# Laying the inputs of a Fourier-plus-experts kernel out in the order in which it loads them

## The chip, the cores and the metric

The kernel runs on one core of a Trainium2 chip. The metric is the device time of one execution in microseconds (us), as the median of several runs without a profile. A profiled execution gives the page and the trace from which the views below are read; its times are us from the start of its span unless they are marked ns.

## What is computed

A two-dimensional Fourier transform over sequence and channels, of which the real part is kept, and then a mixture of experts in which each token goes to one expert. Cut to what matters:

```python
# x: (8, 2496, 256), w_gate: (256, 8), w1: (8, 256, 1024), w2: (8, 1024, 256), all float32
X = np.fft.fft(x, axis=1)
X = np.fft.fft(X, axis=2)
t = X.real.astype(np.float32).reshape(8 * 2496, 256)      # 19968 tokens

logits = t @ w_gate
expert = np.argmax(logits, axis=1)
gate = softmax(logits)[token, expert]
for e in range(8):                                        # every token to its own expert
    h = np.maximum(t[expert == e] @ w1[e], 0.0)
    y[expert == e] = h @ w2[e]
out = gate[:, None] * y
```

## The kernel before

The sequence of 2496 is split as 104 x 24. A batch goes through these steps.

1. **First stage** (`first`). The 24 samples of a row are worked on as 12 pairs of mirrored samples in three thirds of four. For each third, `xl` (four samples) is loaded directly by SP, and `xh` (the four mirrored ones) comes by a gather from GpSimd, because the mirrored rows run backwards and need computed row numbers. VectorE adds the two, with one of them read backwards along the channels, folds the channels into a cosine and a sine half, and TensorE multiplies with `w1` waves. ScalarE copies the results out of PSUM, and SP stores them to the DRAM tensor `Td`.
2. **Regrouping** (`regroup`). Two loads per batch bring `Td` back with other rows on the partitions (120 of them), as `t4`.
3. **Second stage** (`second`). Small matmuls on `t4`, then the channel transform, which gives rows of tokens and their logits.
4. **Routing** (`route`). VectorE finds each token's expert and place; GpSimd scatters the rows to `Xs`, which is sorted by expert: ten scatters of 128 rows for each half of a batch.
5. **Experts** (`experts`). Blocks of 512, 256 or 128 rows of one expert are loaded with that expert's `w1` and `w2` (1 MB each), multiplied, and scattered to the output.

The order of instructions on each engine is written by hand: generators are woven so that the stages of batch b + 1 lie among the experts' work on batch b. Each engine does its own instructions in that order.

The parts that the change touches, with cuts marked:

```python
    ix = cp.tile([NA, B, NQ], I32, name="ix")              # row numbers for the gathers
    pool.iota(ix[:], [[S // 4, B], [-1, NQ]], base=NB // 4 * NA - 1, channel_multiplier=-(NB // 4))
    # ... cut ...
    xall = x.rearrange("b (p j) d -> (b p) j d", j=NB)
    xrows = x.rearrange("b (n j) d -> (b n) (j d)", j=4)

    def load_x(b, q):
        xl = xp.tile([NP, 4, D], F32, tag="xl", name="xl", bufs=3)      # NP = 112
        xh = xp.tile([NA, 4, D], F32, tag="xh", name="xh", bufs=3)      # NA = 104, D = 256
        n = NP if b + 1 < B else NA
        nc.sync.dma_start(out=xl[0:n], in_=xall[NA * b:NA * b + n, 4 * q + 1:4 * q + 5])
        pool.indirect_dma_start(
            out=xh[:].rearrange("p j d -> p (j d)"), out_offset=None, in_=xrows,
            in_offset=bass.IndirectOffsetOnAxis(ap=ix[:, b, q:q + 1], axis=0))
        return xl[0:NA], xh[:]

    def fold(xl, xh, q):
        n = 3 if q == NQ - 1 else 4
        a, m = xl, xh
        vec.tensor_tensor(free(a, 1, [D, n], [1, D - 1]), free(a, 1, [D, n], [1, D - 1]),
                          free(m, 3 * D + D - 1, [-D, n], [-1, D - 1]), op=ALU.add)
        yield
        vec.tensor_tensor(free(a, 0, [D, n]), free(a, 0, [D, n]), free(m, 3 * D, [-D, n]), op=ALU.add)
        fold_d(m, a, 4)
        yield

    def load(b, q):                    # the loads of third q; with q = 0 sample 0 too, as x0
        # ... cut ...

    def first(b):
        pm0 = xp.tile([NA, D], F32, tag="pm0", name="pm0")
        for q in range(NQ + 1):        # NQ = 3
            # ... first half of the fold of third q; yield ...
            # ... half of the matmuls of third q - 1; second half of the fold; yield ...
            if q:
                half1(b, q - 1, 1, pm, pm0, t1)
                nc.sync.dma_start(out=Td[b][:, 4 * (q - 1) * D:4 * q * D], in_=t1[:].rearrange("p j d -> p (j d)"))
                load(b + 1, q - 1)
            next(f, None)
            if q == 1:
                fold_d(pm0[:], ahead.pop((b, "x0")), 1)
            pm = xh
            yield

    def regroup(b, h):
        t4 = sp.tile([GP, HALF, D], F32, tag="t4", name="t4")           # GP = 120, HALF = 6
        n = min(HALF, NG - h * HALF)
        nc.sync.dma_start(
            out=t4[:, 0:n], in_=bass.AP(Td[b].tensor, Td[b].offset + h * HALF * GP * D,
                                        [[D, GP], [GP * D, n], [1, D]]))
        ahead[b, "t4", h] = t4

    # in fetch: a block's rows, then its weights, all on SP
        w1_sb = bp.tile([128, 2, F], F32, tag="w1", name="w1_sb", bufs=3)
        nc.sync.dma_start(out=w1_sb[:], in_=w1[ds(ev, 1)].rearrange("o (c p) f -> p (o c) f", p=128))
        w2_sb = bp.tile([128, FC, D], F32, tag="w2", name="w2_sb", bufs=3)
        nc.sync.dma_start(out=w2_sb[:], in_=w2[ds(ev, 1)].rearrange("o (c p) d -> p (o c) d", p=128))

    # the start of the program
    act.dma_start(out=con["w1"][:, 0:4], in_=waves[:, 0:4])
    load(0, 0)
    act.dma_start(out=con["w1"][:, 4:], in_=waves[:, 4:])
    for _ in range(WARM):              # WARM = 12 matmuls on a tile of ones
        pw = psy.tile([128, D], F32, tag="y", name="py")
        mm(pw[:], ones[:], bc(ones[:], 1, 2))
    load(0, 1)
    load(0, 2)
    act.dma_start(out=con["rt"][:], in_=const_dram("rt", consts["rt"]))
    act.dma_start(out=wg[:], in_=w_gate.rearrange("(c p) e -> p c e", p=128))
    nc.sync.dma_start(out=table[:], in_=const_dram("table", packed))
    nc.sync.dma_start(out=bt[:], in_=const_dram("blocks", cv))
    # ... cut: the rows of padding of Xs; a first Exp ...
    for _ in first(0):
        pass
    regroup(0, 0)
    regroup(0, 1)
    # ... cut: the gate's weights through the channel transform (pg) ...
    early = ahead_of(1)                # first(1), then regroup(1, 0) and regroup(1, 1)
    for _ in range(7):
        next(early)
    for k, _ in enumerate(second(0)):  # second stage and routing of batch 0
        if k % 2 == 0:
            next(early, None)
    # ... cut: experts, woven with the stages of the batches to come ...
```

Of the kernel before, what the change touches and what calls it, by code (L numbers as in the profile page):

```python
# [11 lines left out]
F32 = mybir.dt.float32  # L12
# [33 lines left out]
def free(ap, offset, *dims):  # L46
    return bass.AP(ap.tensor, ap.offset + offset, [list(ap.ap[0])] + [list(d) for d in dims])
# [122 lines left out]


TICKS = 44
WARM = 12
MOST = max(k for now in rounds() for _, k, _ in now)


# [15 lines left out]
def kernel(ctx: ExitStack, tc, x, w_gate, w1, w2, out):  # L192
# [3 lines left out]
    def mm(o, lhsT, rhs, start=True, stop=True, **kw):  # L196
        nc.tensor.matmul(o, lhsT=lhsT, rhs=rhs, start=start, stop=stop, **kw)  # L197
# [39 lines left out]
    ix = cp.tile([NA, B, NQ], I32, name="ix")  # L237
    pool.iota(ix[:], [[S // 4, B], [-1, NQ]], base=NB // 4 * NA - 1, channel_multiplier=-(NB // 4))
    pad = cp.tile([128, W], F32, name="pad")
    vec.memset(pad[:], 0.0)  # L240
    vec.memset(pad[:, D:D + 1], OUT)
# [20 lines left out]
    ident = con["ident"]  # L262
    waves = const_dram("w1", consts["w1"])


    xall = x.rearrange("b (p j) d -> (b p) j d", j=NB)
    xrows = x.rearrange("b (n j) d -> (b n) (j d)", j=4)

    def load_x(b, q):
        xl = xp.tile([NP, 4, D], F32, tag="xl", name="xl", bufs=3)  # L270
        xh = xp.tile([NA, 4, D], F32, tag="xh", name="xh", bufs=3)
        n = NP if b + 1 < B else NA
        nc.sync.dma_start(out=xl[0:n], in_=xall[NA * b:NA * b + n, 4 * q + 1:4 * q + 5])
        pool.indirect_dma_start(  # L274
            out=xh[:].rearrange("p j d -> p (j d)"), out_offset=None, in_=xrows,
            in_offset=bass.IndirectOffsetOnAxis(ap=ix[:, b, q:q + 1], axis=0))
        return xl[0:NA], xh[:]

    def fold_d(o, a, n):

# [2 lines left out]
        vec.tensor_tensor(free(o, H + 1, [D, n], [1, H - 1]), lo, hi, op=ALU.subtract)  # L283
        vec.tensor_copy(free(o, 0, [D, n], [H, 2]), free(a, 0, [D, n], [H, 2]))  # L284

    def fold(xl, xh, q):

        n = 3 if q == NQ - 1 else 4
        a, m = xl, xh
        vec.tensor_tensor(free(a, 1, [D, n], [1, D - 1]), free(a, 1, [D, n], [1, D - 1]),  # L290
                          free(m, 3 * D + D - 1, [-D, n], [-1, D - 1]), op=ALU.add)
        yield
        vec.tensor_tensor(free(a, 0, [D, n]), free(a, 0, [D, n]), free(m, 3 * D, [-D, n]), op=ALU.add)
        fold_d(m, a, 4)
        yield

# [11 lines left out]

    ahead = {}

    def load(b, q):
        if b < B:
            ahead[b, q] = load_x(b, q)
        if b < B and q == 0:
            n = NP if b + 1 < B else NA
            x0 = xp.tile([NP, D], F32, tag="x0", name="x0")
            nc.sync.dma_start(out=x0[0:n], in_=xall[NA * b:NA * b + n, 0])
            ahead[b, "x0"] = x0[0:NA]

    def first(b):  # L320

        pm0 = xp.tile([NA, D], F32, tag="pm0", name="pm0")
        for q in range(NQ + 1):
            f = iter(())
            if q < NQ:
                xl, xh = ahead.pop((b, q))
                f = fold(xl, xh, q)
# [12 lines left out]
            if q == 1:  # L340
                fold_d(pm0[:], ahead.pop((b, "x0")), 1)
            pm = xh
            yield

    base = con["cap"]

    def regroup(b, h):
        t4 = sp.tile([GP, HALF, D], F32, tag="t4", name="t4")
        n = min(HALF, NG - h * HALF)
        nc.sync.dma_start(  # L350
            out=t4[:, 0:n], in_=bass.AP(Td[b].tensor, Td[b].offset + h * HALF * GP * D,
                                        [[D, GP], [GP * D, n], [1, D]]))
        ahead[b, "t4", h] = t4

    zz = cp.tile([128, 2, NW * 128], F32, name="zz")
# [1 line left out]
    def second(b):  # L357

        t4 = None

        def turn_last(h):

            nonlocal t4
            t4 = ahead.pop((b, "t4", h))
            n = min(HALF, NG - h * HALF)
            pr = pm_.tile([GP, HALF], F32, tag="m", name="pr")
            mm(pr[:, 0:n], con["rot"][:], t4[:, 0:n, H])
            act.copy(t4[:, 0:n, H], pr[:, 0:n])

        def group(g):  # L370
            i, n = g % HALF, LAST if g == NG - 1 else GP
            p2 = pm_.tile([128, 2, n], F32, tag="m", name="p2")
            for c in range(2):
                mm(p2[:, c], t4[:, i, c * H:(c + 1) * H], con["m2"][:, c, 0:n])
# [144 lines left out]

    def turn(size, xb):  # L520
# [119 lines left out]
    act.dma_start(out=con["rt"][:], in_=const_dram("rt", consts["rt"]))  # L640
    act.dma_start(out=wg[:], in_=w_gate.rearrange("(c p) e -> p c e", p=128))
    nc.sync.dma_start(out=table[:], in_=const_dram("table", packed))
    nc.sync.dma_start(out=bt[:], in_=const_dram("blocks", cv))
    sent(unordered(nc.sync.dma_start(
        out=Xs[E * CAP:].rearrange("(k p) w -> p k w", k=BLK // 128), in_=bc(pad[:], 1, BLK // 128)), "xs"), 0)
# [5 lines left out]
    todo = in_order()  # L651
    for _ in first(0):
        pass
    regroup(0, 0)
    regroup(0, 1)
    vec.tensor_copy(tri[:], con["tri"][:])
    for c in range(2):
        pg = pm_.tile([128, E], F32, tag="m", name="pg")
# [36 lines left out]
_OUTS = [((NT, D), "float32")]  # L695


# [18 lines left out]
```

## Time and profile before

| | before |
|---|---|
| time, median of 3 runs | 1383.64 us (1382.79 to 1387.59) |
| profiled execution | 1424.57 us, span 1422.8 us |
| TensorE matmul (PE) busy | 1338.3 us (94%) |
| TensorE weight load (PEld) busy | 1016.2 us (71%) |
| VectorE (DVE) busy | 382.6 us (27%) |
| ScalarE (ACT) busy | 283.8 us (20%) |
| GpSimd (POOL) busy | 350.8 us (25%) |
| moved by DMA | 248.81 MB in 134,517 packets |

The profile is read in three steps: the table of windows tells which engine limits which stage; the chain that ended last tells what that engine waited for; the groups by tile and the timeline give the length of one instruction and the distance to the next. A name such as `xh<-in_x_dram,ix` says that `xh` is written from the input `x` and the row numbers `ix`. PE is TensorE's matmul and PEld its weight load, which overlap. In the page's list of DMA issues, a load of `xl` is 448 KB, one of weights 1024 KB, one of `t4` 720 or 600 KB, the waves `w1` 182 and 500.5 KB, the table 493.5 KB and `rt` 256 KB.

### The profile page before, as it was taken

How to read it: one execution, taken by the hardware profiler on the slowest of the kernel's cores; microseconds unless marked ns; L12 is line 12 of the kernel's file. 1: busy time of each engine (PE TensorE's matmuls, PEld its weight loads, DVE VectorE, ACT ScalarE, POOL GpSimd, SP SyncE). 2: the span in 40 equal slices, each digit the busy share in tenths (PEclk: the TensorE clock that was granted, in tenths of full speed). 3: DMA queues.
4: the chain of work that ended last, by engine and by line, in shares of the span. 5: the costliest groups of instructions: out<-in, count | busy, mean ns of one | idle time of the engine just before them, and what ended most of it. 6: DMA issues, size and time to landing. Idle time of an engine off the chain costs nothing.

```text
span 1422.8 us, 17245 instructions
## 1 busy us (share of the span) xinstructions
PE 1338.3 (94%) x6186; PEld 1016.2 (71%) x6186; DVE 382.6 (27%) x1206; ACT 283.8 (20%) x656; POOL 350.8 (25%) x360
## 2 busy tenths in 40 slices
PE   4658798998999999999999999999999999999998
PEld 3557687776676667776676667776667779999997
DVE  3453243333242222322132321333211111111111
ACT  1322122132132211221122211221111111111111
POOL 1243314333314311234113311224221111111111
PEclk9768899999999999999999999999999999999999
DMA  8859777644546452561435342333442248788883
GB/s 228 204 184 291 242 240 235 246 135 117 209 131 206 135 173 90 179 187 64 168 105 166 131 175 89 108 111 107 168 143 93 89 136 269 264 265 267 268 272 102
DMA packets 134517, 248.81 MB, mean 175 GB/s; under 512 B 11245, under 2 KB 93839, under 8 KB 134432
## 3 DMA queue, kind: packets, MB, share of 16 engines
q1 hardware_dynamic: 114438, 194.38, 42.8%
q0 software_dynamic: 19344, 52.37, 10.8%
q10 hardware_dynamic: 650, 0.97, 0.3%
q8 instruction: 49, 0.80, 0.2%
q14 instruction: 36, 0.29, 0.1%
HBM read 194.28 MB, written 54.83 MB: 175 GB/s over the span
## 4 chain that ended last, share of the span: by engine, by line
PE 55%; issue 31%; POOL 5%; another core or an unknown queue 3%; DMA 2%; DVE 2%; ACT 1%; POOLq 0%; SPq 0%; DVEq 0%; ACTq 0%
PE py L197 22%; PE ph L197 22%; PE p L197 6%; POOL out_dram L212 4%; PE s L197 3%; PE pt L528 1%; DMA xh<-in_x_dram,ix 1%; POOL Xs L212 1%; DMA Td<-t 1%; DMA t<-Td 0%; DVE hT L570 0%; DVE rows L406 0%; DMA xb<-Xs 0%; POOLq L212 0%
## 5 line engine op out<-in xcount | busy, mean ns | idle before, releaser
L197 PE MATMUL ph<-xT,w_sb 128*128 128x512 f32 (+2 forms) x2112 | 589.3, 433 | 7.7 <-ACT hT L572 2.3
L197 PE MATMUL py<-w_sb,hT 128*128 128x256 f32 x2608 | 584.6, 381 | 8.5 <-DVE hT L570 8.5
L197 PEld LDWEIGHTS py<-w_sb,hT 128*128 128x128 f32 x2608 | 489.4, 191 | 72.1 <-DVE hT L570 9.3
L197 PEld LDWEIGHTS ph<-xT,w_sb 128*128 128x128 f32 x2112 | 340.2, 192 | 205.3 <-issue 176.5
L212 POOL DMA_INDIRECT out_dram<-y,ro x163 | 159.2, 977 | 861.7 <-ACT y L585 832.5
L570 DVE TENSOR_SCALAR hT<-ph 128x512 f32<-128x512 f32 x163 | 112.7, 692 | 716.6 <-issue 350.5
L585 ACT ACTIVATE y<-py,xb 128x256 f32<-128x256 f32 x163 | 77.3, 474 | 625.0 <-PE py L197 537.5
L212 POOL DMA_INDIRECT Xs<-rows,pi x160 | 159.1, 994 | 122.8 <-issue 76.1
L572 ACT ACTIVATE hT<-ph 128x512 f32<-128x512 f32 x163 | 97.3, 597 | 324.1 <-PE ph L197 287.7
L529 DVE TENSOR_SCALAR xT<-pt,table 128x512 f32<-128x512 f32 (+1 forms) x94 | 63.3, 674 | 66.7 <-PE pt L528 63.8
L197 PE MATMUL s<-xh,w 104*112 104x256 f32 (+2 forms) x208 | 62.0, 424 | 17.6 <-DVE xh L284 13.9
L197 PEld LDWEIGHTS p<-table,t 120*128 120x128 f32 x352 | 56.8, 211 | 29.2 <-issue 19.8
L197 PE MATMUL p<-table,zz 128*128 128x145 f32 (+1 forms) x320 | 60.0, 315 | 15.7 <-issue 8.0
L197 PE MATMUL p<-table,t 120*128 120x120 f32 (+1 forms) x352 | 59.6, 296 | 11.1 <-issue 4.1
L404 DVE COPY lg<-p 128x16 f32<-128x16 f32 x80 | 14.0, 175 | 203.8 <-ACT zs L401 148.0
L197 PEld LDWEIGHTS p<-table,zz 128*128 128x128 f32 x320 | 48.7, 207 | 20.0 <-issue 11.1
L197 PEld LDWEIGHTS s<-xh,w 104*112 104x112 f32 x208 | 39.8, 205 | 30.3 <-DVE xh L284 15.1
L528 PEld LDWEIGHTS pt<-table,xb 128*128 128x128 f32 x326 | 40.7, 142 | 17.7 <-issue 11.6
L528 PE MATMUL pt<-table,xb 128*128 128x128 f32 x326 | 51.6, 274 | 1.7 <-DMA xb<-Xs 1.7
L406 DVE SCALAR_TENSOR_TENSOR rows<-p,zs 128x129 f32<-128x129 f32 x160 | 48.4, 344 | 1.6 <-issue 0.6
L274 POOL DMA_INDIRECT xh<-in_x_dram,ix x24 | 24.3, 1014 | 80.4 <-PE s L197 59.8
L375 ACT COPY zz<-p 128x240 f32<-128x240 f32 (+1 forms) x88 | 31.1, 353 | 54.1 <-PE p L197 36.8
(84 smaller groups left out, 333.1 us busy)
## 6 DMA issues: line engine op xcount, KB each, us to landing
w_sb<-in_moe_w_dram SPq DMA_DIRECT2D x132, 1024.0 KB
xb<-Xs SPq DMA_DIRECT2D x28, 516.0 KB
Td<-t SPq DMA_DIRECT2D x24, 448.0 KB
xl<-in_x_dram SPq DMA_DIRECT2D x21, 448.0 KB
t<-Td SPq DMA_DIRECT2D x8, 720.0 KB
t<-Td SPq DMA_DIRECT2D x8, 600.0 KB
xb<-Xs SPq DMA_DIRECT2D x13, 258.0 KB
xb<-Xs SPq DMA_DIRECT2D x25, 129.0 KB
```

The source lines that it names most:

```text
L197: nc.tensor.matmul(o, lhsT=lhsT, rhs=rhs, start=start, stop=stop, **kw)
L212: return unordered(pool.indirect_dma_start(out=dst, out_offset=bass.IndirectOffsetOnAxis(ap=idx, axis=0), in_=rows, in_offset=None, bounds ...
L274: pool.indirect_dma_start(out=xh[:].rearrange("p j d -> p (j d)"), out_offset=None, in_=xrows, in_offset=bass.IndirectOffsetOnAxis(ap=ix[: ...
L375: act.copy(zz[:, :, g * GP:g * GP + n], p2[:])
L404: vec.tensor_copy(lg[:, k:k + 2], p3[:, NY:NY + 2 * E].rearrange("p (m e) -> p m e", m=2))
L406: vec.scalar_tensor_tensor(rows[:, k + m, 0:NY], p3[:, 0:NY], zs[:, 0:1], zs[:, 1:], op0=ALU.add, op1=op)
L528: nc.tensor.transpose(pt[:, c, t], xb[:, 2 * h + t, c * 128:(c + 1) * 128], ident[:])
L529: vec.tensor_scalar(xT[:, :, 256 * h:256 * h + 128 * n], pt[:].rearrange("p c t k -> p c (t k)"), con["alt"][:], None, op0=ALU.mult)
L570: vec.tensor_scalar(o, ph[:], 0.0, None, op0=ALU.max)
L572: act.activation(o, ph[:], ACTF.Relu)
L585: act.activation(y[:, i], py[:], ACTF.Copy, scale=xb[:, i, D + 1:D + 2])
```

## The change

The inputs are laid out anew before the kernel runs, so that each load reads one run of memory per partition, and the start loads what it needs in the order in which it needs it.

- **x**: a third of a batch is now one block of 104 rows of 8 KB: four samples and, beside them, the four mirrored ones, already reversed in rows and channels. One load of 112 partitions on SP takes the place of the direct load and the gather. Sample 0 sits in the free place of the last third, so its own load goes too. The add becomes one instruction on contiguous columns.
- **Weights**: `w1`, `w2` and the gate's weights are laid out with the partition outermost, so that a partition's 8 KB of an expert's `w1` or `w2` are one run; before, `w1` came in runs of 4 KB and `w2` in runs of 1 KB.
- **Regrouping**: `t4` has 128 partitions; the last eight are not used.
- **Batch 0**: on SP first its three loads of x with the second part of the waves among them, then the table, `rt` and the gate's weights. Batch 1 is not loaded during the first stage of batch 0 but after it: two thirds ahead of the regrouping loads of batch 0, the last behind them, and then the small tables. The stores to `Td` of batches 0 and 1 go out on ScalarE's queue instead of SP's.
- 16 warm-up matmuls in place of 12.

The diff, cut to its core:

```diff
-WARM = 12
+WARM = 16
 ...
-    def load_x(b, q):
-        ...
+    def load(b, q):
+        if b < B:
+            xq = xp.tile([NP, 8, D], F32, tag="xq", name="xq", bufs=3)
+            row = (b * NQ + q) * NA
+            nc.sync.dma_start(out=xq[:].rearrange("p j d -> p (j d)"), in_=x[row:row + NP])
+            ahead[b, q] = xq[0:NA]
 ...
-    def fold(xl, xh, q):
-        ...
+    def fold(xq, q, pm0):
+        a, m = xq[:, 0:4], xq[:, 4:8]
+        n = 4
+        if q == NQ - 1:
+            n = 3
+            fold_d(pm0, m[:, 3], 1)
+        vec.tensor_tensor(a[:, 0:n], a[:, 0:n], m[:, 0:n], op=ALU.add)
+        yield
         fold_d(m, a, 4)
         yield
 ...
                 half1(b, q - 1, 1, pm, pm0, t1)
-                nc.sync.dma_start(out=Td[b][:, 4 * (q - 1) * D:4 * q * D], in_=t1[:].rearrange("p j d -> p (j d)"))
-                load(b + 1, q - 1)
+                (nc.sync if b > 1 else act).dma_start(out=Td[b][:, 4 * (q - 1) * D:4 * q * D], in_=t1[:].rearrange("p j d -> p (j d)"))
+                if b:
+                    load(b + 1, q - 1)
             next(f, None)
-            if q == 1:
-                fold_d(pm0[:], ahead.pop((b, "x0")), 1)
-            pm = xh
+            pm = xq[:, 4:8]
             yield
 ...
-        t4 = sp.tile([GP, HALF, D], F32, tag="t4", name="t4")
+        t4 = sp.tile([128, HALF, D], F32, tag="t4", name="t4")
 ...
-                                        [[D, GP], [GP * D, n], [1, D]]))
+                                        [[D, 128], [GP * D, n], [1, D]]))
 ...
-        nc.sync.dma_start(out=w1_sb[:], in_=w1[ds(ev, 1)].rearrange("o (c p) f -> p (o c) f", p=128))
+        nc.sync.dma_start(out=w1_sb[:], in_=w1[ds(ev, 1)].rearrange("o p c f -> p (o c) f"))
 ...
-        nc.sync.dma_start(out=w2_sb[:], in_=w2[ds(ev, 1)].rearrange("o (c p) d -> p (o c) d", p=128))
+        nc.sync.dma_start(out=w2_sb[:], in_=w2[ds(ev, 1)].rearrange("o p c d -> p (o c) d"))
 ...
     act.dma_start(out=con["w1"][:, 0:4], in_=waves[:, 0:4])
     load(0, 0)
-    act.dma_start(out=con["w1"][:, 4:], in_=waves[:, 4:])
+    load(0, 1)
+    nc.sync.dma_start(out=con["w1"][:, 4:], in_=waves[:, 4:])
+    load(0, 2)
+    nc.sync.dma_start(out=table[:], in_=const_dram("table", packed))
+    nc.sync.dma_start(out=con["rt"][:], in_=const_dram("rt", consts["rt"]))
+    nc.sync.dma_start(out=wg[:], in_=w_gate)
     for _ in range(WARM):
         ...
-    load(0, 1)
-    load(0, 2)
-    ... rt, wg, table, bt and the padding of Xs, loaded here
 ...
     for _ in first(0):
         pass
+    load(1, 0)
+    load(1, 1)
     regroup(0, 0)
     regroup(0, 1)
+    load(1, 2)
+    ... bt and the padding of Xs, loaded here
 ...
+    inputs = laid(**inputs)            # the new layout of x, w_gate, w1 and w2
```

More of the change, by code (lines that the diff above doesn't have):

```diff
@@ L235 @@
     psy = ctx.enter_context(tc.tile_pool(name="psy", bufs=2, space=PSUM))
-    ix = cp.tile([NA, B, NQ], I32, name="ix")
-    pool.iota(ix[:], [[S // 4, B], [-1, NQ]], base=NB // 4 * NA - 1, channel_multiplier=-(NB // 4))
     pad = cp.tile([128, W], F32, name="pad")
@@ L263 @@
     waves = const_dram("w1", consts["w1"])
-    xall = x.rearrange("b (p j) d -> (b p) j d", j=NB)
-    xrows = x.rearrange("b (n j) d -> (b n) (j d)", j=4)
-    def load_x(b, q):
[L270 to L277, printed above, removed]
+    def load(b, q):
[4 more added lines that the diff above has]
+            ahead[b, q] = xq[0:NA]
     def fold_d(o, a, n):
@@ L284, in fold_d @@
         vec.tensor_copy(free(o, 0, [D, n], [H, 2]), free(a, 0, [D, n], [H, 2]))
-    def fold(xl, xh, q):
[L288 to L291, printed above, removed]
+    def fold(xq, q, pm0):
[5 more added lines that the diff above has]
+        vec.tensor_tensor(a[:, 0:n], a[:, 0:n], m[:, 0:n], op=ALU.add)
         yield
-        vec.tensor_tensor(free(a, 0, [D, n]), free(a, 0, [D, n]), free(m, 3 * D, [-D, n]), op=ALU.add)
         fold_d(m, a, 4)
@@ L309 @@
     ahead = {}
[L311 to L318, printed above, removed]
     def first(b):
@@ L325, in first @@
             if q < NQ:
-                xl, xh = ahead.pop((b, q))
-                f = fold(xl, xh, q)
+                xq = ahead.pop((b, q))
+                f = fold(xq, q, pm0[:])
             next(f, None)
@@ L366, in turn_last @@
             pr = pm_.tile([GP, HALF], F32, tag="m", name="pr")
-            mm(pr[:, 0:n], con["rot"][:], t4[:, 0:n, H])
-            act.copy(t4[:, 0:n, H], pr[:, 0:n])
+            mm(pr[:, 0:n], con["rot"][:], t4[0:GP, 0:n, H])
+            act.copy(t4[0:GP, 0:n, H], pr[:, 0:n])
         def group(g):
@@ L373, in group @@
             for c in range(2):
-                mm(p2[:, c], t4[:, i, c * H:(c + 1) * H], con["m2"][:, c, 0:n])
+                mm(p2[:, c], t4[0:GP, i, c * H:(c + 1) * H], con["m2"][:, c, 0:n])
             act.copy(zz[:, :, g * GP:g * GP + n], p2[:])
@@ L637 @@
         mm(pw[:], ones[:], bc(ones[:], 1, 2))
-    load(0, 1)
-    load(0, 2)
[L640 to L645, printed above, removed]
     warm = cp.tile([1, 1], F32, name="warm")
@@ L653 @@
         pass
+    load(1, 0)
+    load(1, 1)
     regroup(0, 0)
     regroup(0, 1)
+    load(1, 2)
+    nc.sync.dma_start(out=bt[:], in_=const_dram("blocks", cv))
+    sent(unordered(nc.sync.dma_start(
+        out=Xs[E * CAP:].rearrange("(k p) w -> p k w", k=BLK // 128), in_=bc(pad[:], 1, BLK // 128)), "xs"), 0)
     vec.tensor_copy(tri[:], con["tri"][:])
@@ L695, with laid @@
 _OUTS = [((NT, D), "float32")]
+def laid(x, moe_w_gate, moe_w1, moe_w2):
+    n1, i = np.arange(NA)[:, None], np.arange(4)[None]
+    back = -np.arange(D) % D
+    thirds = []
+    for q in range(NQ):
+        s = NB * n1 + 4 * q + 1 + i
+        far = x[:, -s % S][..., back]
+        if q == NQ - 1:
+            far[:, :, 3] = x[:, ::NB]
+        thirds.append(np.concatenate([x[:, s], far], 2))
+    xs = np.stack(thirds, 1).reshape(-1, 8 * D)
+    xs = np.concatenate([xs, np.zeros((NP - NA, 8 * D), np.float32)])
+    return {
+        "x": xs,
+        "moe_w_gate": moe_w_gate.reshape(2, 128, E).transpose(1, 0, 2),
+        "moe_w1": moe_w1.reshape(E, 2, 128, F).transpose(0, 2, 1, 3),
+        "moe_w2": moe_w2.reshape(E, FC, 128, D).transpose(0, 2, 1, 3),
+    }
 def kernel(**inputs):
```

## The prediction, made before the changed kernel was seen

> **What bounds the kernel now.** I first cut the span into stages with the table of busy time by window, because the shares on the page average over stages with different limits. Its columns: span, busy time of PE, PEld, DVE, ACT and POOL (instructions in brackets), granted TensorE clock, busy share of the 16 DMA engines, GB/s.
>
> ```profile
> 0.00:45.00 45.00, 18.53 (x60) 12.43 (x60) 17.16 (x45) 6.17 (x10) 7.56 (x12) 0.85 0.87 220
> 45.00:100.00 55.00, 35.65 (x188) 30.60 (x187) 28.70 (x130) 18.23 (x56) 24.93 (x23) 0.69 0.63 182
> 100.00:330.00 230.00, 203.03 (x1068) 170.41 (x1069) 78.90 (x279) 53.57 (x136) 77.03 (x78) 0.94 0.75 234
> 330.00:1400.00 1070.00, 1063.98 (x4763) 787.09 (x4763) 255.61 (x749) 203.17 (x450) 238.39 (x244) 1.00 0.49 162
> 1400.00:1422.80 22.80, 17.14 (x112) 15.63 (x110) 2.27 (x6) 2.62 (x5) 2.92 (x3) 0.95 0.22 79
> ```
>
> From 330 to 1400 us TensorE is busy 1063.98 of 1070 us at full clock, with DMA half idle. Nothing done to loads, VectorE or GpSimd can shorten that stage. PE's idle time is 26.5 us in the first 45, 19.4 us in the next 55, 27 us from 100 to 330, and 5.7 us at the end. The change can only win there, and mostly in the first 100 us, before the experts start.
>
> Next I followed the chain that ended last through that start (start, length, what).
>
> ```profile
> 3.24 15.78 DMA xh<-in_x_dram,ix
> 19.04 1.22 DVE xl L290
> ...
> 28.85 0.59 ACT t L307
> 29.46 8.56 DMA Td<-t
> 38.04 6.57 DMA t<-Td
> 44.74 0.54 PE pr L197 x2
> ...
> 72.01 5.15 another core or an unknown queue
> 77.18 0.17 ACT t L368
> 77.35 4.11 another core or an unknown queue
> ...
> 100.79 1.99 PE ph L197 x8
> ```
>
> The first second stage (`pr`) starts at 44.74 us, and 31 us of the way there are three DMA waits: the mirrored gather of x (15.78), the last third's store to Td (8.56) and the regrouping load (6.57). While this goes on the DMA engines are the bound: the windows 0:10 and 10:20 show shares 0.82 and 0.99 at 190 and 243 GB/s.
>
> The third view is the tile Xs from 60 to 95 us (instruction, minimum/median/maximum ns, first and last start).
>
> ```profile
> L212 POOL DMA_INDIRECT Xs<-rows,pi x20: 974/977/1847, 63.4 to 90.4; - x20
> ```
>
> Between the second stage and the experts stands GpSimd: twenty scatters of batch 0, 1.28 us from start to start, 63.4 to 91.6 us with three slow ones. The load of the first block's rows follows at 93.5 (DMA issues of SP), and `ph` starts at 100.8. This part is a series of fixed lengths behind 44.7 us; if its start moves, all of it should move.
>
> The profiled run took 1424.57 us, the unprofiled median is 1383.64. The unexplained waits in the chain up to 400 us (5.15, 4.11, 16.55, 8.71, 2.40, 5.80) sum to 42.7 us, about the 40.9 us difference, and in several of them PE, ACT and DVE stand still together. I read them as a cost of profiling and count no gain from removing them. That is a choice.
>
> **What the Trainium skill says.** (1) "DMA: Bandwidth & Descriptors", section "Issuing engines are not separate DMA queues": DMAs of SP, ACT and GpSimd interleave on the same 16 engines. The trace agrees: the first gather was issued at 1.75 us, and the first add, which waits for it, starts at 14.99 us, because three thirds of x, 683 KB of waves, the table and `rt` share the engines with it. (2) The same page, section "Why a DMA increments its semaphore by 16 and not by 1": a DMA is split over the largest number up to 16 that divides its outer size; by this 120 partitions use 15 engines, 104 use 13, 112 and 128 use 16. No view here shows the split; it decides little below. (3) "TensorE: Matmul & The Clock Gate", Part 1: after an idle window the array runs at half clock. The trace agrees: 0.50 in windows 40:50 and 70:80. More warm-up matmuls (16 for 12) are over by 5 us, and PE idles again after them.
>
> **The change part by part.**
>
> *First load in order of use.* Up to 14.99 us the engines moved about 190 x 10 + 243 x 5 = 3.1 MB; at a steady 243 GB/s the 0:10 window implies 2.2 us before the first byte. Afterwards the first add needs 182 KB of waves and one load of 112 x 8 KB = 917 KB: 1.10 MB, so 2.2 + 4.5 = 6.7 us, about 7 with the landing. The second load follows 3.8 us later (10.8), the other waves (0.51 MB) at 12.9, the third load at 16.7.
>
> *Folds.* The add was 1215 ns plus a 158 ns column add; now one add of 1024 columns, an estimated 1.22 us from the first figure. Saved: 24 x 0.16 = 3.8 us of VectorE, which is 27% busy: nothing on the path. The 0.5 us fold of sample 0 moves ahead of the third add. The third fold therefore takes 2.4 (before: 22.05 to 24.40) + 0.5 = 2.9 us and ends at 19.6.
>
> *Matmuls and store.* In before, from that fold's end to the last copy's end took 5.0 us, with PE still busy with the previous third; I take 4.5. The last store is issued at 24.1 instead of 29.46: 5.4 us earlier. Its wait was 8.56 us because batch 1's loads were already queued. Now only load(1,0) and part of load(1,1) are. The store goes out on ACT's own queue and shares the engines half and half: 2 x 0.459 MB / 243 = 3.8 us, plus an estimated 1.7 us at the ends, so 5.5. It lands at 29.6 instead of 38.0: 8.4 earlier.
>
> *Regroup.* 128 rows for 120 on 16 engines for 15: 6.7% more bytes over 6.7% more engines, no change. The load is 0.79 MB: 3.2 us plus 2 for the ends plus about 1 for what remains of load(1,1), 6.2 against 6.57. `pr` starts near 36 instead of 44.74: 8.8 us earlier. With 300 GB/s for the longer 8 KB rows (the windows 100:110 and 110:120 reach 323 GB/s on weights) each step shrinks and it comes to 11 to 12. I take 10.
>
> *From there on.* The second stage, the routing and the twenty scatters keep their lengths. The 24 gathers of xh leave GpSimd (1014 ns each, 24.3 us), but none lies among the twenty scatters of batch 0; later GpSimd is a quarter busy. So `ph` starts about 10 us earlier, the order of PE's work before and after it is the same, and the end moves by the same 10 us.
>
> *Batch 1 later.* Its third load is issued behind both regroupings and lands near 38 us. The seventh step of the first stage of batch 1 puts an add that waits for it into VectorE's order ahead of the second stage of batch 0. The first VectorE work there came 7.7 us after `pr` (52.41 against 44.74), so at 43.7: a margin of some 5 us, no cost.
>
> *Weights.* w2 came in runs of 1 KB, now 8 KB per partition. In the packet records a 1024-byte packet takes 46 ns (median), one of 4096 bytes 159 ns, that is 45 against 39 ns per KB. A 1 MB load needs 1024 x 46 / 16 = 2.9 us of all engines, afterwards by the second rate an estimated 2.5: 0.4 x 66 = 26 us of engine time, in stages where TensorE is the bound. On the path I count 1 to 2 us, for the long issues that full queues cause on SP (6.34 us for a Td store at 98.4, 6.51 us for the regroup loads at 131.5).
>
> Sum: 1383.6 - 10 - 1.5 = 1372.
>
> **The rivals.** *A: the start's gain is lost on the way.* If batch 1's delayed third load stops VectorE, or ACT, which now issues stores, is held by them, the scatters do not start earlier. For it: engines work in order, and SP's stores did take up to 6.3 us to issue. Against it: the margin above, and those long issues came with weights in the queue, which ACT's stores of batches 0 and 1 precede. It would make 1380 to 1385. *B: the DMA engines are the bound up to 330 us, and longer runs and fewer packets give back much of the 27 us idle there.* For it: share 0.75 in that stage and 1.06 around 110 us. Against it: the idle time there coincides with the unexplained waits that I gave to profiling. It would make 1350 to 1360. *C: slower, because one SP queue in order makes each transfer wait for the one before.* For it: table and `rt` now wait for 3.4 MB. Against it: they are needed only after the last store. It would make 1388.
>
> **Range and chances.** The start gives 9 to 12 us, the weights 0 to 3, A takes most of it away, B adds up to 15: 1357 to 1381. 2% is 27.7 us, below 1356; only B reaches it. Faster 0.09, same 0.89, slower 0.02.
>
> **What would show it.** In the changed profile: first add near 7 us; last Td store issued near 24; `pr` near 36 us; first scatter of Xs near 53 and the first `ph` near 90; PE busy time within 10 us of 1338, all saving in idle time before 100 us; 330 to 1400 unchanged. A first scatter still after 60 us proves A. An unchanged start with fewer idle us from 100 to 330 and an unprofiled gain over 20 us proves B.

## The result, and the profile after

| | before | after | ratio, 95% interval |
|---|---|---|---|
| time, median | 1383.22 us (1381.86 to 1387.59, 4 runs) | 1371.94 us (1369.63 to 1372.80, 4 runs) | 0.991 [0.9885, 0.9936] |

The change gains 11.3 us, 0.9%: clear of the noise and small. It is time of the device alone: the new layout is made by numpy on the host before the kernel starts, and what that costs is not in it. The prediction was 1372.0. The sum held; what stood behind several of its terms did not, as the experiments show.

The table of windows of the kernel after (columns as in the prediction: span, busy PE, PEld, DVE, ACT, POOL, clock, DMA share, GB/s):

```profile
0.00:45.00 45.00, 28.77 (x113) 21.30 (x114) 18.90 (x48) 11.06 (x25) 0.20 (x4) 0.81 0.92 271
45.00:100.00 55.00, 34.65 (x197) 29.27 (x196) 33.05 (x143) 16.96 (x50) 21.88 (x20) 0.75 0.66 223
100.00:330.00 230.00, 226.79 (x1192) 184.17 (x1191) 89.01 (x309) 60.01 (x150) 82.73 (x85) 1.00 0.69 242
330.00:1350.00 1020.00, 1019.90 (x4604) 760.13 (x4603) 238.28 (x680) 194.00 (x427) 218.06 (x224) 1.00 0.46 166
```

TensorE is idle for 16.2 us of the first 45 where before it was idle for 26.5, and it does 113 matmuls there instead of 60. From 330 us on it is busy for 1019.90 of 1020 us: this stage is as full as it was. The line of 100 to 330 us looks like a gain of some 24 us over the first trace of before, and is none: the trace of e1 below, which has before's x and before's order, has TensorE busy for 226.69 us there too. The first trace of before came from an execution with long unexplained waits, to which I come back.

The timeline of the kernel after, cut to the steps of the start (start, length, engine, line, operation, out<-in; in brackets the idle time ahead of it and what ended it):

```profile
7.40 1.22 DVE L285 TENSOR_TENSOR xq<-xq 104x1024 f32<-104x1024 f32 x1 [6.10 <-DMA xq<-in_x_dram]
...
24.85 1.07 ACT L300 COPY t<-s 112x512 f32<-112x512 f32 x2 [8.49 <-DMA Td<-t]
...
25.95 0.31 ACTq L321 DMA_DIRECT2D Td<-t  x1
...
29.07 0.98 SPq L333 DMA_DIRECT2D t<-Td  x2
...
33.94 0.56 PE L197 MATMUL pr<-t,table 120*120 120x6 f32 x2 [1.15 <-DMA t<-Td]
...
38.92 0.29 DVE L274 TENSOR_TENSOR pm<-xq 104x127 f32<-104x127 f32 x1 [7.42 <-DMA xq<-in_x_dram]
...
87.89 3.75 PE L197 MATMUL ph<-xT,w_sb 128*128 128x256 f32 x8 [1.95 <-DMA w_sb<-in_moe_w_dram]
```

The first add starts at 7.40 us (before: 14.99), the last store to Td is issued at 25.95 (29.46), the regrouping loads at 29.07 (38.04), `pr` starts at 33.94 (44.74) and the first `ph` at 87.89 (100.79). The two waits on the way, store and regrouping load, have shrunk from 8.6 and 6.7 us to 3.1 and 4.9 (start to start).

The tile Xs from 40 to 95 us, and two links of the chain that ended last, both of the kernel after:

```profile
L212 POOL DMA_INDIRECT Xs<-rows,pi x20: 971/976/1780, 52.8 to 79.5; - x20
```

```profile
79.48 2.39 DMA Xs<-rows,pi
...
82.70 5.05 DMA w_sb<-in_moe_w_dram
```

The twenty scatters run from 52.8 instead of 63.4 us, at the same distance from each other, and after the last of them the first block waits for its rows and then 5.05 us for its weights.

### The profile page after: what moved, and what is told of

It reads as the page before. It is cut to its first block, busy times and chain, and to the rows that moved or that the text cites. A ratio compares the mean times of both kernels' runs of the same rounds, so it can differ in the third digit from the quotient of the medians.

```text
span 1367.9 us, 17145 instructions
## 1 busy us (share of the span) xinstructions
PE 1323.7 (97%) x6190; PEld 1007.3 (74%) x6190; DVE 381.1 (28%) x1182; ACT 284.2 (21%) x656; POOL 325.8 (24%) x335
## 3 DMA queue, kind: packets, MB, share of 16 engines
q10 hardware_dynamic: 885, 2.94, 0.6%
## 4 chain that ended last, share of the span: by engine, by line
PE 53%; issue 31%; POOL 7%; DMA 2%; DVE 1%; POOLq 0%; ACT 0%; SPq 0%; ACTq 0%; DVEq 0%
PE py L197 23%; PE ph L197 22%; POOL out_dram L212 5%; PE p L197 4%; PE s L197 2%; POOL Xs L212 2%; PE pt L511 2%; DMA Xs<-rows,pi 1%; DMA xb<-Xs 1%; DMA Xs<-pad,ti 0%; DMA w_sb<-in_moe_w_dram 0%; POOLq L212 0%; PE rk L197 0%; DVE hT L553 0%; DVE rows L389 0%
## 5 line engine op out<-in xcount | busy, mean ns | idle before, releaser
L197 PE MATMUL s<-xq,w 104*112 104x256 f32 (+2 forms) x208 | 59.5, 409 | 12.8 <-DVE xq L276 12.6
L387 DVE COPY lg<-p 128x16 f32<-128x16 f32 x80 | 13.9, 174 | 181.6 <-ACT zs L384 181.4
L197 PE MATMUL p<-table,zz 128*128 128x145 f32 (+1 forms) x320 | 56.2, 300 | 2.6 <-DVE rows L389 1.4
L197 PEld LDWEIGHTS s<-xq,w 104*112 104x112 f32 x208 | 38.3, 198 | 25.0 <-DVE xq L276 9.3
L197 PEld LDWEIGHTS p<-table,zz 128*128 128x128 f32 x320 | 45.9, 196 | 6.2 <-issue 2.4
L300 ACT COPY t<-s 112x512 f32<-112x512 f32 x48 | 27.9, 584 | 52.2 <-PE s L197 43.6
```

The source lines that it names most:

```text
L300: act.copy(t1[:, 2 * half:2 * half + 2], ps[:])
```

## The experiments

They ran on three chips, here A, B and C. On B every kernel is some 20 to 27 us slower, so a time is set only against the runs of before on its own chip: 1384.59 us on A (25 runs), 1411.05 on B (7 runs), 1384.02 on C (11 runs).

| run | chip | median us (range, runs) | against before, 95% |
|---|---|---|---|
| e1: new layout of the experts' weights alone | A | 1383.51 (1381.02 to 1386.95, 12) | 0.9995 [0.9984, 1.0005] |
| e2: after with the old weights | A | 1370.71 (1370.32 to 1371.78, 4) | 0.9902 [0.9886, 0.9919] |
| e3: after with before's order | A | 1372.35 (1369.73 to 1373.73, 4) | 0.9916 [0.9899, 0.9933] |
| e4: before with after's order | A | 1380.35 (1376.92 to 1386.36, 14) | 0.9975 [0.9963, 0.9987] |
| e5: before once more | B | 1409.34 (1 run) | - |
| e6: x by two loads on SP | B | 1395.46 (1392.67 to 1398.34, 4) | 0.9877 [0.9826, 0.9927] |
| e7: one of the two on GpSimd | B | 1391.70 (1387.28 to 1400.91, 4) | 0.9846 [0.9791, 0.9901] |
| i1: three buffers for `t1` | B | 1391.32 (1390.28 to 1393.02, 4) | 0.9858 [0.9811, 0.9905] |
| after once more | C | 1370.63 (1369.72 to 1372.64, 6) | 0.9905 [0.9889, 0.9921] |
| e8: e3 once more | C | 1372.77 (1371.46 to 1374.01, 6) | 0.9917 [0.9902, 0.9933] |
| i2: first block's weights ahead of its rows | C | 1369.05 (1367.65 to 1371.14, 5) | 0.9890 [0.9873, 0.9908] |
| i3: i2 and warm-up matmuls | C | 1369.30 (1368.48 to 1371.26, 5) | 0.9898 [0.9880, 0.9916] |

And the same steps in each trace, from the timelines (us; store: the last of batch 0's three stores to Td issued; scatter: the first one to Xs; the last column is the span less the start of the first `ph`):

| run | first add | store | regroup | `pr` | scatter | `ph` | span | rest |
|---|---|---|---|---|---|---|---|---|
| e1 (A) | 14.85 | 28.40 | 37.66 | 44.31 | 62.36 | 100.25 | 1381.3 | 1281.0 |
| e4 (A) | 13.98 | 27.74 | 32.26 | 38.61 | 56.97 | 94.79 | 1378.5 | 1283.7 |
| e3 (A) | 7.40 | 23.65 | 29.88 | 35.19 | 53.12 | 88.71 | 1367.9 | 1279.2 |
| e8 (C) | 7.64 | 24.88 | 32.68 | 39.15 | 57.57 | 93.10 | 1372.2 | 1279.1 |
| e2 (A) | 8.46 | 26.76 | 30.52 | 35.37 | 54.19 | 89.25 | 1369.0 | 1279.8 |
| after | 7.40 | 25.95 | 29.07 | 33.94 | 52.78 | 87.89 | 1367.9 | 1280.0 |
| after once more (C) | 7.95 | 26.59 | 29.73 | 34.67 | 55.22 | 90.32 | 1369.4 | 1279.1 |
| e5 (B) | 14.97 | 28.81 | 37.06 | 43.55 | 60.65 | 98.26 | 1407.6 | 1309.3 |
| e7 (B) | 12.76 | 27.85 | 32.68 | 37.57 | 56.24 | 93.92 | 1399.1 | 1305.2 |
| e6 (B) | 8.74 | 25.80 | 29.55 | 34.61 | 55.05 | 92.59 | 1396.3 | 1303.7 |

The last column is the first finding. On A and C, and in the trace of after, what follows the first `ph` takes 1279.1 to 1281.0 us whatever was changed, but for 1283.7 in e4. Nearly the whole gain is an earlier first `ph`: 100.25 - 87.89 = 12.4 of the 1381.3 - 1367.9 = 13.4 us of span from e1 to after. On B the stretch behind the first `ph` is longer and shrinks too, from 1309.3 to 1303.7 and 1305.2.

Two traces of one kernel also differ: after by 0.7 us at `pr` and 2.4 at `ph`, e3 and e8 by 4.0 and 4.4. The first adds of kernels that load x alike, in one load on SP, lie within 1.1 us of each other. So a difference of 2 or 3 us at `pr` or `ph` between two single traces shows nothing by itself.

### e1 and e2: the weights

e1 is before with this, e2 is after with the opposite:

```diff
-        nc.sync.dma_start(out=w1_sb[:], in_=w1[ds(ev, 1)].rearrange("o (c p) f -> p (o c) f", p=128))
+        nc.sync.dma_start(out=w1_sb[:], in_=w1[ds(ev, 1)].rearrange("o p c f -> p (o c) f"))
-        nc.sync.dma_start(out=w2_sb[:], in_=w2[ds(ev, 1)].rearrange("o (c p) d -> p (o c) d", p=128))
+        nc.sync.dma_start(out=w2_sb[:], in_=w2[ds(ev, 1)].rearrange("o p c d -> p (o c) d"))
```

> The kernel before with only w1 and w2 laid out in 8 KB runs. Theory (the gain is an earlier start of the experts): no change without a profile, 1380 to 1386 us. Rival (fewer packets and longer runs feed engines that are full up to 330 us): at least half of the 11.3 us, so 1378 or less. Of the profile: the changed kernel's profiled run took 1369.6 us, no longer than its unprofiled ones, where the kernel before took 41 us longer with a profile. If the unexplained waits come from the profiler and the number of packets (134,517 before, 63,089 after), this kernel, with about 67,000, is profiled at 1390 or less; if they come from the start's order or the gathers, it is still profiled at 1410 or more.

> The changed kernel with w1 in runs of 4 KB and w2 in runs of 1 KB as before. Theory: 1371 to 1375 us without a profile, first scatter to Xs still at 52 to 54 us, the first block's ph within 1 us of 87.9. Rival (weights): 1377 or more. Of the profile: if packets make the profiled run long, 1405 to 1420 us with waits on unexplained queues in the chain; if not, 1369 to 1376.

Runs of 8 KB instead of 1 and 4 KB are worth nothing here: 0.9995 with an interval that holds 1, and after without them is as fast as after. The 1 to 2 us that I had put on the path for them are not there. The thought that many small packets make the unexplained waits of a profiled execution fell as well: the profiled execution of e2, with its 1 KB runs, took 1370.74 us, among its unprofiled ones.

e1 also serves as an undisturbed trace of before. The chain that ended last, in e1 (start, length, what):

```profile
1.75 13.08 DMA xh<-in_x_dram,ix
...
28.40 9.24 DMA Td<-t
37.66 6.51 DMA t<-Td
...
93.18 6.93 DMA w_sb<-in_moe_w_dram
100.25 3.75 PE ph L197 x8
```

It has the same three waits at the start as the first trace of before, and no unexplained wait anywhere.

### e3, e4 and e8: layout against order

e3 (and e8, which is the same kernel on another chip) is after with before's order of use; the new layout of x and the weights, the 128 partitions and the 16 warm-up matmuls stay. Its core:

```diff
-                (nc.sync if b > 1 else act).dma_start(out=Td[b][:, 4 * (q - 1) * D:4 * q * D], ...)
-                if b:
-                    load(b + 1, q - 1)
+                nc.sync.dma_start(out=Td[b][:, 4 * (q - 1) * D:4 * q * D], ...)
+                load(b + 1, q - 1)
 ...
-    load(1, 0)
-    load(1, 1)
     regroup(0, 0)
     regroup(0, 1)
-    load(1, 2)
```

with `rt`, the gate's weights and the second part of the waves back on ScalarE's queue. e4 is before with these lines the other way round, so that the gathers and the old layout stay.

> The changed kernel with the order of the start as before: waves, rt and gate weights on ACT, batch 1 loaded during the first stage of batch 0, stores to Td on SP; the new layout of x and weights stays. Theory (order of use makes the earlier start): the last Td store waits for batch 1's loads again, pr after 40 us, first scatter after 58 us, 1377 to 1383 us. Rival (one contiguous load in place of two, without the gather, makes it): pr by 36, 1371 to 1374.

> The kernel before, with the gathers and the layout of before, but batch 0 in order of use: batch 1 not loaded during its first stage, stores of batches 0 and 1 on ACT. Theory (order): first add near 11 us because the gathers of all three thirds still share the engines with the direct loads, pr near 37, first scatter near 56, 1374 to 1379 us. Rival (layout): within 3 us of before, 1380 to 1386.

> The layout-only kernel (order of the start as before) on the same chip as the changed kernel. If the order of use is worth nothing once the gathers are gone: within 1.5 us of it. If it is worth the 4 us that it gave alone: 3 to 5 us slower.

The layout alone gives 12.2 us on A and 11.3 on C, the order alone 4.2. Together that is 16.5, against 13.4 for the whole on C (after against before) and 13.9 on A (e2, which lacks only the weights, for which e1 shows nothing). The intervals reach some 2 us to either side, so that the times alone don't prove the shortfall. On top of the layout the order is worth 1372.77 - 1370.63 = 2.1 us on C, which is neither of the two cases that were expected of e8. The ranges overlap, and the intervals against before too; set against each other, the two groups of six differ by 1.9 us in the mean with a standard error of 0.6, so a small gain is likely.

Two lines of the timeline of e4 say what the order does and what it doesn't:

```profile
13.98 1.22 DVE L290 TENSOR_TENSOR xl<-xl,xh 104x1020 f32<-104x1020 f32 x1 [12.68 <-DMA xh<-in_x_dram,ix]
...
38.61 0.54 PE L197 MATMUL pr<-t,table 120*120 120x6 f32 x2 [3.56 <-DMA t<-Td]
```

It hardly moves the first add (14.85 to 13.98). It shortens the store's landing, from 37.66 - 28.40 = 9.26 us in e1 to 32.26 - 27.74 = 4.52, and so `pr` starts 5.7 us earlier. (e4 also moves the stores to ScalarE's queue, so that the order of the loads and the queue of the stores are not told apart.) Three links of the chain of e3 show the other half:

```profile
23.65 6.14 DMA Td<-t
29.88 5.27 DMA t<-Td
...
83.56 5.02 DMA w_sb<-in_moe_w_dram
```

With the layout alone the store waits 6.14 us (7.70 in e8) although batch 1's loads are queued beside it, the regrouping load 5.27 (6.43). In after the store lands in 3.1 us, but it is issued 2.3 us later than in e3, so that of some 3 us gained on the landing about 1 is left at the regrouping. It is issued later because TensorE had waited 4.49 us for the fold of the last third and ran its next six matmuls in 2.62 us at a granted clock of 0.62 and 0.52 (windows 20:22 and 22:24 of after), where in e3 they took 1.52 us at 1.00. So the two parts work in part at the same wait. How far they overlap stays open: between the two traces of C the order is worth 4.5 us at `pr`, between e3 and after 1.25.

### e5, e6 and e7: why the first add is early

e6 is after, but loads a third of x by two DMAs of 4 KB per partition on SP; e7 puts the second of them on GpSimd's queue, as a plain load. e5 is before, unchanged, on the same chip.

```diff
-            nc.sync.dma_start(out=xq[:].rearrange("p j d -> p (j d)"), in_=x[row:row + NP])
+            nc.sync.dma_start(out=xq[:, 0:4].rearrange("p j d -> p (j d)"), in_=x[row:row + NP, 0:4 * D])
+            pool.dma_start(out=xq[:, 4:8].rearrange("p j d -> p (j d)"), in_=x[row:row + NP, 4 * D:8 * D])   # e6: nc.sync
```

> The kernel before, unchanged, profiled once more, because the kernel with only new weights was profiled at 1383 us and showed none of the waits on unexplained queues. If those 41 us belong to that one profiled execution: 1380 to 1388 us with a profile, no such waits in the chain, first add at 14 to 16 us, ph near 100 us. If they belong to this program under a profile: 1415 or more again.

> The changed kernel with each third of x loaded by two direct loads on SP, 4 KB runs each, in place of one with 8 KB runs. The order-only kernel gained 4 us, the layout-only kernel 12. Theory now (what cost was the gather, whose first packets moved only about 10 us after the start): as the changed kernel, 1370 to 1374 us, first add by 8.5 us. Rival (run length and number of loads): first add after 10 us, 1375 or more.

> The changed kernel with the mirrored half of each third loaded by a direct load that GpSimd issues (4 KB runs, no row numbers), the other half by SP. If it is GpSimd's queue that is late beside a full SP queue, the first add comes after 11 us and the time is 1374 to 1380 us; if only the indirect form is late, first add by 9 us and 1370 to 1374 us.

The first add in the timeline of e6:

```profile
8.74 1.23 DVE L286 TENSOR_TENSOR xq<-xq 104x1024 f32<-104x1024 f32 x1 [7.45 <-DMA xq<-in_x_dram]
```

and in that of e7, with the issue of GpSimd's loads:

```profile
1.29 1.79 POOL L269 DMA_DIRECT2D xq<-in_x_dram  x3 [0.83 <-POOLq L714]
...
12.76 1.22 DVE L286 TENSOR_TENSOR xq<-xq 104x1024 f32<-104x1024 f32 x1 [11.46 <-DMA xq<-in_x_dram]
```

The DMA queues of e7 from 4 to 6 us and, below it, from 6 to 8 us (packets, MB, share of the 16 engines; q1 is SP's queue, q0 GpSimd's):

```profile
q1 hardware_dynamic: 132, 0.49, 97.3%
...
q0 software_dynamic: 1, 0.00, 0.8%
```

```profile
q1 hardware_dynamic: 67, 0.24, 51.7%
q0 software_dynamic: 59, 0.24, 51.4%
```

The length of the runs is not what matters for the first add: 8.74 us with two runs of 4 KB, against 8.35 with one of 8 KB in i1 on the same chip. Who issues the load is: 4.0 us of the add's 6.2 between e5 and e6 are the step from GpSimd's plain load to SP's, and 2.2 more the step from the gather to the plain load together with the new order. GpSimd issues its load at 1.29 us, and the packet records have the first packet of its queue at 5.48 us and the next at 6.10; SP issues its first load at 0.76 and has its first packet at 1.99. The gather's packets begin at 7.83 us in e1 and at 6.16 in e4, so the "about 10 us" in the expectation of e6 was too late. Once GpSimd's packets move, they take half of the engines' time and SP's later loads the other half. The 4.0 us hold both, a late start and a shared rate, and these runs don't divide them. The Trainium skill, page "DMA: Bandwidth & Descriptors", section "Latency and other measured facts", gives the first byte of a load from GpSimd about 1 us and of one from SP about 0.6; the runs agree in the sign, but from issue to first packet e7 has 4.2 us for GpSimd and 1.2 for SP, beside the other loads at the start of this program.

What this delay is worth in time these runs don't settle. `pr` starts at 43.55 in e5, 37.57 in e7, 34.61 in e6, so that 3.0 of 8.9 us at `pr` belong to the issuer; at `ph` it is 1.3 of 5.7. Of the times e7's median is even the lower one, 1391.70 against 1395.46 with overlapping ranges, on a chip whose runs of before reach from 1404.40 to 1417.14.

### i1: is the wait of the copies on the path?

In after, ScalarE's last copies wait 8.49 us for a store to leave `t1` (24.85 in the timeline above), though the batch's third store is what everything waits for next.

```diff
-                t1 = xp.tile([NP, 4, D], F32, tag="t1", name="t1")
+                t1 = xp.tile([NP, 4, D], F32, tag="t1", name="t1", bufs=3)
```

> The changed kernel with three t1 buffers instead of two. In its trace ScalarE's copies of the last third wait until 24.85 us for the first store to Td (8.49 us idle), while the matmuls of their first half end near 22. Theory (this wait is on the path): last store issued 1.5 to 3 us earlier, pr near 32, ph near 86, 1368 to 1371 us. Rival (the stores then share the engines with load(1,1) and land no earlier): pr unchanged within 0.7 us, 1371 to 1373 us.

The timeline of i1:

```profile
20.93 2.87 PE L197 MATMUL s<-xq,w 104*112 104x256 f32 x6 [2.16 <-issue]
...
25.54 0.59 ACT L300 COPY t<-s 112x512 f32<-112x512 f32 x1 [1.97 <-PE s L197]
...
26.16 0.31 ACTq L321 DMA_DIRECT2D Td<-t  x1
```

The copies no longer wait for the store, they wait for TensorE, which takes 2.87 us for the first six matmuls of the last third (e3: 1.52) and is not done with that third before 25.5 us. The store is issued at 26.16, 0.66 us behind TensorE, and `pr` starts at 34.43: nothing is gained against after. In after TensorE was done with the third at 24.3 us and the store was issued at 25.95. So by estimate (24.3 + 0.66 = 25.0) only some 1 us of the 8.49 us of visible waiting was on the path, because the next limit stood close behind. After itself was not run on B, so that the times don't decide it.

The next limit is not always there. In e7, on the same chip and with two buffers, the six matmuls took 1.52 us and the last third was done at 24.2 us, but the copies stood until the store had left `t1`:

```profile
26.75 1.07 ACT L301 COPY t<-s 112x512 f32<-112x512 f32 x2 [4.53 <-DMA Td<-t]
```

The store was issued at 27.85, so that by the same estimate some 3 us were on the path there. A third buffer for that case was not tried.

### i2 and i3: the wait for the first weights

In after the first block's rows are loaded ahead of its weights, and the weights can only be issued when the last scatter has landed, because SP works in order. i2 issues the weights of the first block first; i3 adds 24 matmuls on ones ahead of its first `pt`, so that TensorE should be warm.

```diff
+        if not ahead_w:
+            rows()
         nc.sync.dma_start(out=w1_sb[:], in_=w1[ds(ev, 1)].rearrange("o p c f -> p (o c) f"))
         nc.sync.dma_start(out=w2_sb[:], in_=w2[ds(ev, 1)].rearrange("o p c d -> p (o c) d"))
+        if ahead_w:                    # the first block only
+            rows()
 ...
+                for _ in range(24):    # i3 only
+                    pw = psy.tile([128, D], F32, tag="y", name="py")
+                    mm(pw[:], ones[:], bc(ones[:], 1, 2))
```

> The changed kernel unchanged, as the base of the three runs beside it. Chips differ: where the kernel before takes 1383 to 1385 us this one takes 1370 to 1373; where it takes some 1411, theory says the gain is the earlier start plus what waits on unexplained queues vanish, 1385 to 1400. First scatter at 52 to 54 us, first ph within 1 us of 88 on either.

> The changed kernel, with the first block's weights issued ahead of its rows. In its trace the first ph waits for w1 until 87.89 us (1.95 us idle), while xT was ready at 86.7; weights need no scattered rows. Theory: first ph near 86.7, 0.5 to 1.5 us faster than the changed kernel. Rival (the rows then land later, behind 2 MB): no gain or up to 2 us slower.

> As the one with weights ahead, and 24 bf16 matmuls on ones in PE's idle time before the first block's transposes (77.9 to 84.8 us). There the granted clock was 0.50 from 80 to 90 us, and the first eight ph took 3.75 us where later ones take 1.9. Theory: clock 1.00 when ph starts, another 1.5 to 3 us, in all 2 to 4 us faster than the changed kernel. Rival (what follows waits for DMA anyway): no gain over weights ahead alone.

After's own second trace missed what was expected of it by a little: first scatter at 55.22 us and first `ph` at 90.32. The timeline of i2, and below it that of after on the same chip:

```profile
87.51 1.12 PE L518 MATMUL pt<-table,xb 128*128 128x128 f32 x4 [6.95 <-DMA xb<-Xs]
...
89.47 3.78 PE L197 MATMUL ph<-xT,w_sb 128*128 128x256 f32 x8 [0.84 <-DVE xT L519]
```

```profile
87.56 1.12 PE L511 MATMUL pt<-table,xb 128*128 128x128 f32 x4 [7.25 <-DMA xb<-Xs]
...
90.32 3.64 PE L197 MATMUL ph<-xT,w_sb 128*128 128x256 f32 x8 [1.65 <-DMA w_sb<-in_moe_w_dram]
```

`ph` no longer waits for the weights but for its own transposed rows, 2.0 us behind `pt` instead of 2.8: 0.8 us. The 5.05 us link of the chain was mostly time in which the rows were on their way too. At 1369.05 us i2 has the best median of all, 1.6 us under after on the same chip with overlapping ranges; that it beats after is likely, and not shown.

The windows of i3 around its extra matmuls, which ran from 78.58 to 83.40 us:

```profile
82.00:84.00 2.00, 1.40 (x9) 0.65 (x7) 0.00 (x0) 0.00 (x0) 0.00 (x0) 1.00 0.15 37
84.00:86.00 2.00, 0.40 (x2) 0.40 (x3) 0.00 (x0) 0.00 (x0) 0.00 (x0) 0.79 0.52 138
86.00:88.00 2.00, 1.16 (x5) 0.76 (x4) 0.82 (x2) 0.00 (x0) 0.00 (x0) 0.50 1.00 357
```

The clock (third figure from the end) did rise to 1.00, and was back at 0.50 when `ph` came at 87.56 us. The Trainium skill, page "TensorE: Matmul & The Clock Gate", Part 1, says that some 3.4 us of work raise the clock and an idle window of some 3.4 us lowers it. The run agrees with the first, with 4.8 us of work. It lowers the clock sooner than the second: TensorE stood still for 2.20 us, up to `pt` at 85.60, and the clock was gone by 86 us, at most 2.6 us after the last of the extra matmuls. The first eight `ph` took 3.78 us as ever, and 1369.30 is no better than i2.

### The unexplained waits and chip B

I had read the waits without a releaser in before's first trace as a cost of profiling. The runs speak against that. On B the unprofiled runs of before are slow as well (1411.05), the profiled one (1409.34) among them, with 5.30 and 9.75 us of such waits in its chain; on A and C profiled and unprofiled executions agree (e1 stands in for before there, with 1383.12 us profiled and 1383.51 in the median; before itself was profiled on B and in its first trace, whose chip is not on record), and the chains of all eight traces from there have none. That the first trace came from a chip such as B is likely, and not shown. The changed kernel has them on B too. From the chain of i1:

```profile
132.94 14.25 another core or an unknown queue
```

In that stretch VectorE stands still for 14.27 us before an `hT` while GpSimd issues twelve scatters in a row (131.87 to 147.5 us). In after GpSimd does the same from 124.35 to 141.3 us, and VectorE's `hT` in it waits only for TensorE. e6 and e7 stall before an `hT` on B as well, for 14.25 and 14.30 us. Why one chip stalls there and others don't stays open.

## Why the prediction was right, and where it was not

- **The bound.** It held on A and C. From the first `ph` on nothing moved (1279 to 1281 us, 1283.7 in e4), and all but about 1 us of the gain lies before it. Rival B (the DMA engines up to 330 us) fell: e2 with old weights is as fast, and of the idle time from 100 to 330 us, 27 us in the first trace of before, e1 has 3.3. Rival C (slower, 1388) fell with the time. On B the idle time of that stage is 22.2 us in e5 and 16.1 in i1; what part of the gain there comes from it stays open.
- **"First load in order of use."** The size was right (about 7 us predicted, 7.40 measured), the cause only in part. I worked out how many bytes stand ahead of the first add and let 243 GB/s carry them. Bytes do stand ahead, on full engines: up to the first add the packets carry 3.21 MB in e1 and 1.56 in after. But the sum had 1.10 MB, so that it came out right by chance, and it took the order of issue to be what puts the others ahead. e4 has the order; its add comes at 13.98, behind 2.94 MB. e3 has before's order; its add comes at 7.40, behind 1.49. What moves it is that no part of it comes through GpSimd's queue (e7 against e6: 4.0 us). My reading of the skill's sentence on shared engines led there: that the gather was issued at 1.75 us and needed at 14.99 I took for sharing alone, where in e1 its packets begin only at 7.83 and share the engines from then on.
- **Folds.** The third fold ends at 20.1 us (19.6). VectorE's busy time falls by 1.5 us, not 3.8, and as said none of it is on the path.
- **"Matmuls and store."** Issued at 25.95 instead of 24.1, landed after 3.1 us instead of 5.5. The step failed in both terms and was right in the sum, 29.07 against 29.6. The first term was too small because the matmuls run at a clock of 0.62 and 0.52 there; the second too long because I let the store share the engines half and half, where from 25.95 to 29.07 us ScalarE's queue has 56.6% of the engines' time and SP's 10.8%. That batch 1's queued loads lengthened this wait fits e4, which halves it, together with the stores on ScalarE's queue.
- **Regroup.** 4.9 us instead of 6.2; `pr` at 33.94 instead of 36.
- **"From there on" and rival A.** Scatter at 52.78 (53), `ph` at 87.89 (90). VectorE did stop for batch 1's third load, 7.42 us up to 38.92 as the timeline shows, and was ready again within the margin: its first work of the second stage, `lg`, comes at 41.70 us, 7.8 us behind `pr`, where it was 7.7 in before. But the part after the scatters did not keep its length: from first scatter to `ph` 37.9 us in e1, 37.8 in e4, 35.1 to 35.6 in e2, e3, e8 and both traces of after. The wait for the first weights makes most of it (6.93 and 7.54 against 4.81 to 5.05 us). This is a gain of some 2 us that the sum didn't have. I take it for the quieter DMA engines in that stretch without having isolated it; on chip B, all without gathers, e6 and e7 show 37.5 and 37.7, and i1 35.5.
- **"Weights."** Mis-sized: 1.5 us predicted, 0 measured (e1, e2). It stood in for the 2 us of the point above, so the total still came out.
- **TensorE's busy time** was predicted within 10 us of 1338.3 and is 1323.7. The first trace of before was a bad yardstick: e1 has 1322.9.
- **"A cost of profiling."** Not borne out, as told above. It did no harm to the number, since I counted no gain from it, and that choice was right.

Not tried, and so open: the stores on SP alone, the regrouping on 120 partitions, and the 12 warm-up matmuls, each by itself in the changed kernel. e3's 11 to 12 us belong to the layout with the last two.

## What to carry to other kernels

Before the first dependent work of a program starts, ask which engine issues each part of its input, and not only how many bytes stand ahead of it: the first add came 4 us later with half of its bytes on GpSimd's queue than with all on SP's, though these runs don't settle what that is worth in the total. Two changes that shorten the same wait need not add up, so test each alone and both together before sharing out the gain. And take a second trace of the kernel before, on another chip, ahead of reading its unexplained waits: 27 us of idle time that looked like a stage to gain in were 3.3 us on A (e1) and 22.2 on B (e5).

## What was not expected of the hardware

- A plain load issued by GpSimd at 1.29 us had its first packet at 5.48 us, and the add that needs it started 4.0 us later than with the same load on SP (12.76 against 8.74 us), at the start of the program.
- TensorE's clock fell from 1.00 to 0.50 around an idle time of 2.20 us (i3, 83.40 to 85.60).
- In the layout of the weights, runs of 1 KB and of 8 KB gave the same time (0.9995 [0.9984, 1.0005]), with 132 loads of 1 MB, in a kernel that TensorE bounds.
- The same kernel took 1384 us on two chips and 1411 on a third, where single stalls of VectorE last up to 14.30 us.
